# Four blocks instead of two share the opening phase of an attention and MoE kernel, with two sets of partial sums in DRAM

## The chip, the cores and the metric

One core of one Trainium2 chip runs the program. The metric is the device time of one execution in microseconds (us). PE is TensorE, DVE is VectorE, ACT is ScalarE, POOL is GpSimd, and SP is the engine whose queue issues most DMAs.

## What is computed

Attention over keys and values that are averaged in groups of 8 (576 positions become 72), then a dense two-layer MLP, then a mixture of 8 experts, of which each token uses the best one. Cut to what matters:

```
k_p, v_p = k.reshape(B,H,72,8,D).mean(3), v.reshape(B,H,72,8,D).mean(3)
x = softmax(q @ k_p.T / 8) @ v_p            # (8,8,576,64), as 4608 tokens x 512
h = x @ w_in                                # 512 -> 2048
y = maximum(0.01*h, h) @ w_out              # 2048 -> 512
e = argmax(y @ w_gate); p = softmax(y @ w_gate)[e]
out = p * (maximum(y @ w1[e], 0) @ w2[e])   # 512 -> 1024 -> 512
```

The inputs lie in DRAM; the weights `w_in` and `w_out` of the dense layer come as 64-bit floats.

## The kernel before

The 4608 tokens are cut into 18 blocks of 256 (`b`), and the 2048 columns of the dense layer into 16 pieces of 128 (`f`). A **slot** is one pair (b, f). The list `seq` sets the order of the slots, and each engine executes its instructions in program order. A slot `s` holds, in this order:

- `g1(b, f)`: 12 matmuls of 256 columns (x and weights are each split in a high and a low part, three products of the four are used) into a PSUM bank of tag `h`; ACT copies the bank times 0.01 into an SBUF tile `g`; DVE takes the maximum of the two.
- `g_lo` of the slot before (DVE), then what `hooks` planned for this slot (`at(slot, function)`): attention steps, key and value pooling, loads, evacuations.
- `g2` of two slots earlier: 6 matmuls of 512 columns into two PSUM banks `y`, which gather all 16 pieces of a block.
- `conv`: conversion of weight pieces. `w_load64` loads 512 KB, `w_conv1` takes 2 ACT and 4 DVE instructions to make fp32 of 64-bit words, `w_conv2` (1 ACT, 1 DVE) splits them into the two parts. There are 32 pieces: `w_in` and `w_out` for each f.
- `g_hi(b, f)` (ACT) makes the high part of the activation; `g_lo` (DVE) the low part.

So `g2` of a slot needs `g_lo`, which stands on DVE behind the maximum of the next slot, and that stands behind the conversion of its own slot.

In the **opening phase** the weights are not yet there. Blocks 0 and 1 go through it together: slots 0 to 3 are (0,0) to (0,3), then (0,f) and (1,f-4) alternate (LAG = 4), and slots 28 to 31 are (1,12) to (1,15). Block b = 2 begins at slot 32, and every later block takes 16 slots. An attention tile `t` (128 tokens) is made by `att_a` (PE transposes, ACT copy), `att_b` (scores; DVE maximum and subtraction), `att_e` (ACT exp), `att_n` (DVE sum, reciprocal, product), `att_c` (PE transposes, ACT and DVE splits); `att_av(b)` (PE, ACT, DVE) makes the block's x. After a block, `y_evac` copies y to SBUF on ACT and stores it to DRAM. Its gate logits are 16 DVE reductions (`logit`); only block 0 uses PE instead (`y_tr`, `y_logit`). From slot 34 on the expert weights are brought in 128 pieces through a ring of three SBUF buffers of tag `ps`: `ps_load` (SP), two slots later `ps_split` (ACT copy, POOL subtraction), one slot later `ps_store` (DMA issued by ACT). The ring hands out its buffers in program order, and a request waits until that buffer's last user is done. The expert steps begin after slot 287.

Of the kernel before, what the change touches and what calls it, by code (L numbers as in the profile page):

```python
# [21 lines left out]
def kernel(  # L22
# [13 lines left out]
    P = 128  # L36
# [3 lines left out]
    LAG = 4  # L40
    E, _, FE = moe2_w1.shape
# [24 lines left out]
    lst = dram.tile([(E * CAP + 1) * P, 2], F32, name="lst")  # L66
    wgT_d = dram.tile([E, DM], F32, name="wgT_d")
# [282 lines left out]
    def att_av(b):  # L350
        for g in range(2):
# [16 lines left out]
            xv = xs(b)  # L368
            act_copy(xv[:, ks, 0], pv)
            sub(nc.vector, xv[:, ks, 1], pv, f32(xv[:, ks, 0]))  # L370


    def w_load64():
        kind, f = w_todo.pop(0)
        r = r64[w_cnt[0] % len(r64)]
        w_cnt[0] += 1
# [39 lines left out]
    w_raw, w_mid, w_cnt = {}, {}, [0]  # L416
# [3 lines left out]
    def g1(b, f):  # L420
        p = pt("h")
        xv = xs(b)
        n = 0
        for kk in range(KD):
            for l, r in ((0, 0), (0, 1), (1, 0)):
                nc.tensor.matmul(  # L426
                    p[:, 0:BLK], win(f)[:, kk, l], xv[:, kk, r], start=(n == 0), stop=(n == 3 * KD - 1)
                )
                n += 1
        t = sb([P, BLK], F32, "g", 2)  # L430
        g = p[:, 0:BLK]
# [13 lines left out]
    def g2(b, f):  # L445
        hl = g_hl.pop((b, f))
        if f == 0:
            for i in range(TPB):
                y_ps[b, i] = bank(f"y{2 * (b == 1) + i}")
        last = f == NF - 1  # L450
        order = [(0, 0, 0), (0, 0, 1), (1, 0, 0), (1, 0, 1), (0, 1, 0), (1, 1, 0)]
        for i, l, r in order:
            nc.tensor.matmul(  # L453
                y_ps[b, i], hl[:, l, i * P:i * P + P], wout(f)[:, r], start=(f == 0 and l + r == 0),
                stop=(last and l == 1),
            )
# [367 lines left out]
    def plan():  # L824
        for t in range(4, NT // P):
# [9 lines left out]
        for b in range(2, NB):  # L835
            at((b - 1) * NF + NF - 1, att_av, b)
        for nb in range(2, B):
# [15 lines left out]
            at(max(use[0] - 6, 0), kv_load, nb, 0)  # L853
            at(use[0] - 5, kv_load, nb, 1)
        for i in range(E * NCH):
            s = 34 + i * 9 // 5
# [3 lines left out]
        for b in range(NB - 1):  # L860
            s = (b + 1) * NF + 1
            lg_at = []
            if b == 0:
                at(30, y_evac, 0)
                at(31, y_tr, 0, 0)
                at(32, y_tr, 0, 1)
                at(33, y_logit, 0)
                r = (34, 36)
            elif b == 1:
                ev, r = 37, (46, 48)  # L870
                lg_at = [38 + j // 2 for j in range(16)]
# [31 lines left out]
    def y_tr(b, i):  # L903
# [3 lines left out]
        tg = (("qT", 1), ("q", 1))[i] if b == NB - 1 else ("kv", 2)  # L907
        yT[i] = sb([P, KD, P], F32, *tg)
# [242 lines left out]
```

## Time and profile before

| | |
|---|---|
| time, median of 3 runs (lowest to highest) | 1575.14 us (1573.2 to 1575.79) |
| the profiled execution: its own time, its span | 1575.01 us, 1573.2 us |
| PE busy, DVE busy, ACT busy, POOL busy | 94%, 59%, 41%, 21% of the span |
| mean granted TensorE clock | 0.977 of full speed |

The time outside the span is 1.8 us. Matmuls are pipelined and the profile models their ends, so a busy PE does not mean a PE at its peak rate.

### The profile page before, as it was taken

How to read it: one execution, taken by the hardware profiler on the slowest of the kernel's cores; microseconds unless marked ns; L12 is line 12 of the kernel's file. 1: busy time of each engine (PE TensorE's matmuls, PEld its weight loads, DVE VectorE, ACT ScalarE, POOL GpSimd, SP SyncE). 2: the span in 40 equal slices, each digit the busy share in tenths (PEclk: the TensorE clock that was granted, in tenths of full speed). 3: DMA queues.
4: the chain of work that ended last, by engine and by line, in shares of the span. 5: the costliest groups of instructions: out<-in, count | busy, mean ns of one | idle time of the engine just before them, and what ended most of it. 6: DMA issues, size and time to landing. Idle time of an engine off the chain costs nothing. (4 is left out here: it accounts for less than half of the span.)

```text
span 1573.2 us, 25017 instructions
## 1 busy us (share of the span) xinstructions
PE 1478.4 (94%) x8778; PEld 1292.1 (82%) x8778; DVE 929.4 (59%) x2393; ACT 643.2 (41%) x1444; POOL 329.6 (21%) x290
## 2 busy tenths in 40 slices
PE   4567899999999999999999999999999999999998
PEld 3456689999898888899889899987888888888886
DVE  6989748978788879877878878653111111111111
ACT  4655544445444454544445444322222222222222
POOL 3000002232332233222222333021111111121111
PEclk8787999999999999999999999999999999999999
DMA  8533035656555555545636554054721331661160
GB/s 208 159 108 102 28 127 174 183 166 196 152 178 170 180 160 184 179 157 166 198 135 198 165 162 160 28 212 160 292 111 48 147 145 41 228 278 46 61 235 22
DMA packets 113280, 238.01 MB, mean 151 GB/s; under 512 B 47589, under 2 KB 55785, under 8 KB 109440
## 3 DMA queue, kind: packets, MB, share of 16 engines
q1 hardware_dynamic: 82208, 139.81, 28.5%
q10 hardware_dynamic: 23328, 76.56, 13.1%
q0 software_dynamic: 7616, 20.01, 3.9%
q8 instruction: 71, 1.16, 0.4%
q14 instruction: 57, 0.47, 0.2%
HBM read 418.44 MB, written 87.38 MB: 322 GB/s over the span
## 5 line engine op out<-in xcount | busy, mean ns | idle before, releaser
L453 PE MATMUL y<-w,ghl 128*128 128x512 f32 x1728 | 464.3, 406 | 0.4 <-DVE ghl L126 0.2
L453 PEld LDWEIGHTS y<-w,ghl 128*128 128x128 f32 x1728 | 311.0, 192 | 56.5 <-DVE ghl L126 1.7
L426 PEld LDWEIGHTS h<-x_t,w 128*128 128x128 f32 x1776 | 237.5, 196 | 58.9 <-issue 21.7
L426 PE MATMUL h<-x_t,w 128*128 128x256 f32 x1776 | 245.6, 289 | 40.8 <-ACT ghl L123 21.4
L126 POOL TENSOR_TENSOR ps<-ps 128x512 f32<-128x512 f32 x128 | 182.7, 1427 | 479.8 <-ACT ps L123 356.5
L473 DVE CUSTOM_DVE_ANT_0 junk<-y,wg 128x512 bf16<-128x512 f32 x256 | 197.9, 773 | 1.9
L426 PEld LDWEIGHTS y<-x_t,w 128*128 128x128 f32 x1488 | 189.6, 188 | 9.4
L426 PE MATMUL y<-x_t,w 128*128 128x256 f32 x1488 | 192.1, 280 | 0.0
L126 DVE TENSOR_TENSOR at_t<-a,at_t 128x512 fp32r<-128x512 f32 x76 | 52.4, 689 | 203.8 <-ACT at_t L123 203.6
L126 DVE TENSOR_TENSOR vm<-a,vm 128x512 fp32r<-128x512 f32 x40 | 27.7, 692 | 199.7 <-ACT vm L123 199.7
L123 ACT ACTIVATE g<-h 128x256 f32<-128x256 f32 x164 | 62.9, 383 | 173.0 <-PE h L426 162.4
L433 DVE TENSOR_TENSOR h<-g,h 128x256 f32<-128x256 f32 x164 | 69.5, 424 | 91.6 <-ACT g L123 91.0
L797 PE MATMUL y<-w,at_t 128*128 128x512 f32 x480 | 120.8, 400 | 1.4 <-ACT at_t L123 0.9
L805 POOL DMA_INDIRECT out_dram<-kv,sidx x40 | 40.3, 1008 | 382.7 <-ACT vm L123 192.3
L797 PE MATMUL y<-w,vm 128*128 128x512 f32 x480 | 120.3, 400 | 0.0
L771 PE MATMUL h<-w,x_t 128*128 128x512 f32 x480 | 118.5, 396 | 0.0
L771 PE MATMUL y<-w,x_t 128*128 128x512 f32 x480 | 118.4, 395 | 0.0
L123 ACT ACTIVATE ghl<-h 128x256 fp32r<-128x256 f32 x164 | 62.7, 382 | 111.3 <-PE y L453 46.7
L797 PEld LDWEIGHTS y<-w,at_t 128*128 128x128 f32 x480 | 88.6, 188 | 22.0 <-ACT at_t L123 1.2
L797 PEld LDWEIGHTS y<-w,vm 128*128 128x128 f32 x480 | 88.7, 188 | 20.1
L771 PEld LDWEIGHTS h<-w,x_t 128*128 128x128 f32 x480 | 88.7, 188 | 18.8 <-DVE x_t L126 0.4
L771 PEld LDWEIGHTS y<-w,x_t 128*128 128x128 f32 x480 | 88.6, 188 | 18.4
(238 smaller groups left out, 1906.4 us busy)
## 6 DMA issues: line engine op xcount, KB each, us to landing
w<-wsp SPq DMA_DIRECT2D x156, 2048.0 KB
wsp<-ps ACTq DMA_DIRECT2D x128, 512.0 KB
ps<-in_moe_w_dram SPq DMA_DIRECT2D x128, 256.0 KB
y_d<-y ACTq DMA_DIRECT2D x18, 512.0 KB
q<-in_q_dram SPq DMA_DIRECT2D x28, 256.0 KB
kv<-in_k_dram SPq DMA_DIRECT2D x24, 288.0 KB
kv<-in_v_dram SPq DMA_DIRECT2D x24, 256.0 KB
ps<-in_moe_w_in_dram SPq DMA_DIRECT2D x8, 512.0 KB
```

The source lines that it names most:

```text
L123: nc.scalar.activation(o, i, AF.Copy, scale=scale)
L126: eng.tensor_tensor(out=o, in0=a, in1=b, op=ALU.subtract)
L426: nc.tensor.matmul(p[:, 0:BLK], win(f)[:, kk, l], xv[:, kk, r], start=(n == 0), stop=(n == 3 * KD - 1))
L433: nc.vector.tensor_tensor(out=g, in0=t, in1=g, op=ALU.max)
L453: nc.tensor.matmul(y_ps[b, i], hl[:, l, i * P:i * P + P], wout(f)[:, r], start=(f == 0 and l + r == 0), stop=(last and l == 1),)
L473: nc.vector.tensor_tensor_reduce(out=jk, in0=y_sb[b][:, i], in1=wg_t[0][:, e], scale=1.0, scalar=0.0, op0=ALU.mult, op1=ALU.add, accum_out ...
L771: nc.tensor.matmul(p, xT2[:, t % 2, kk, l], wlane(lane(t), fh * KD + kk)[:, r], start=(n == 0), stop=(n == 3 * KD - 1))
L797: nc.tensor.matmul(p, d[:, kk, l], wlane(lane(t), 2 * KD + 4 * j + kk)[:, r], start=(j == 0 and n == 0), stop=(j == 1 and n == 11),)
L805: nc.gpsimd.indirect_dma_start(out=out, out_offset=bass.IndirectOffsetOnAxis(ap=sidx[:, t:t + 1], axis=0), in_=o, in_offset=None, bounds_c ...
```

## The change

- `seq`: `pair(0, 8)` runs blocks 0 and 1 through f = 0 to 7 (slots 0 to 15), `pair(2, 16)` runs blocks 2 and 3 through all 16 pieces (slots 16 to 47), then come (0, 8..15) in slots 48 to 55 and (1, 8..15) in slots 56 to 63. From slot 64 (block 4) on the order is that of before.
- `cv_at` sets the slot in which each piece is converted: n = 2 to 9 two in a slot in slots 0 to 3, n = 10 to 15 one in each of slots 4 to 9, none in slots 10 to 14, n = 16 to 31 in slots 15 to 39, eight steps of slots for five pieces. There are 5 load buffers instead of 7, and 3 from n = 18 on.
- The y sums of blocks 0 and 1 after f = 7 are copied to SBUF by ACT and stored to DRAM (`y_part`, slots 13 and 18), loaded again (`part_load`, slots 53 and 61, in the `ps` ring) and added by DVE in `y_evac`.
- The activation of blocks 0 to 3 stays in the SBUF tile `g`, no longer in the PSUM bank `h`.
- Attention tiles 4 to 7 and `att_av(2)`, `att_av(3)` move up into slots 7 to 19. Pooling for batch 1 moves up by 2 to 5 slots.
- Blocks 1 to 3 get their gate logits from PE as block 0 does. `y_tr` takes its tile from the `ps` ring. The expert weights start at slot 42 instead of 34, the gate rows for later blocks are loaded after slot 63 instead of slot 31.

```diff
+
+    def w_load64(n):
+        f, kind = divmod(n, 2)
+        r = r64[n % 5 if n < NK else (n - NK) % 3]
         if kind == 0:
             src = moe_w_in.bitcast(I32)[:, 2 * P * f:2 * P * f + 2 * P].rearrange("(a p) c -> p a c", p=P)
...
-        act_copy(t, g, 0.01)
-        nc.vector.tensor_tensor(out=g, in0=t, in1=g, op=ALU.max)
+        h = p[:, 0:BLK]
+        g = t if b < NQ else h
+        act_copy(t, h, 0.01)
+        nc.vector.tensor_tensor(out=g, in0=t, in1=h, op=ALU.max)
         g_raw[b, f] = g

     def g_hi(b, f):
@@ -444,16 +446,31 @@
...
-        if f == 0:
+        first = f == 0 or (b < 2 and f == NF // 2)
+        last = f == NF - 1 or (b < 2 and f == NF // 2 - 1)
+        if first:
             for i in range(TPB):
-                y_ps[b, i] = bank(f"y{2 * (b == 1) + i}")
-        last = f == NF - 1
...
+                y_ps[b, i], hl[:, l, i * P:i * P + P], wout(f)[:, r], start=(first and l + r == 0),
                 stop=(last and l == 1),
             )
+
+    part = {}
+
+    def y_part(b):
+        if b == 0:
+            part["sb"] = sb([P, 2, TPB, DM], F32, "w03")
+        t = part["sb"][:, b]
+        for i in range(TPB):
+            act_copy(t[:, i], y_ps.pop((b, i)))
+        nc.sync.dma_start(out=part_d[b], in_=t)
+
+    def part_load(b):
+        part[b] = sb([P, TPB, DM], F32, "ps", 3)
+        nc.sync.dma_start(out=part[b], in_=part_d[b])

...
         for i in range(TPB):
-            act_copy(y[:, i], y_ps.pop((b, i)))
+            p = y_ps.pop((b, i))
+            if b in part:
+                nc.vector.tensor_tensor(out=y[:, i], in0=part[b][:, i], in1=p, op=ALU.add)
+            else:
+                act_copy(y[:, i], p)
         nc.scalar.dma_start(
...
     seq = []
-    for i in range(NF + LAG):
-        if i < NF:
-            seq.append((0, i))
-        if i >= LAG:
-            seq.append((1, i - LAG))
-    seq += [(b, f) for b in range(2, NB) for f in range(NF)]
+
+    def pair(b, n):
+        for i in range(n + LAG):
+            if i < n:
+                seq.append((b, i))
+            if i >= LAG:
+                seq.append((b + 1, i - LAG))
+
+    pair(0, NF // 2)
+    pair(2, NF)
+    seq += [(b, f) for b in range(2) for f in range(NF // 2, NF)]
+    seq += [(b, f) for b in range(NQ, NB) for f in range(NF)]
+    slot = {x: s for s, x in enumerate(seq)}
...
-        for t in range(4, NT // P):
+        for t, ss in ((4, (7, 8, 9, 10, 12)), (5, (10, 11, 12, 13, 14)), (6, (12, 13, 14, 14, 16)), (7, (15, 16, 17, 17, 18))):
+            for fn, c in zip((att_a, att_b, att_e, att_n, att_c), ss):
+                at(c, fn, t)
+            at(ss[0], q_load, t + 1)
+        at(15, lambda: x_of.update({2: [sb([P, 2, 2, BLK], F32R, "kv", 2) for g in range(2)]}))
+        at(15, att_av, 2)
+        at(19, att_av, 3)
...
+            if nb == 2:
+                use = [48, 51, 53, 56]
             use += [use[3] + 2, use[3] + 4, use[3] + 6]
...
         for i in range(E * NCH):
-            s = 34 + i * 9 // 5
+            s = 42 + i * 9 // 5
...
-            elif b == 1:
-                ev, r = 37, (46, 48)
-                lg_at = [38 + j // 2 for j in range(16)]
+            if b < NQ:
+                e = slot[b, NF - 1] + 3
+                if b != 1:
+                    at(e, y_evac, b)
+                at(e + 1, y_tr, b, 0)
+                at(e + 2, y_tr, b, 1)
+                at(e + 3, y_logit, b)
+                r = (e + 4, e + 6)
+                if b < 2:
+                    at(slot[b, NF // 2 - 1] + 3, y_part, b)
+                    at(e - 5, part_load, b)
...
-        yT[i] = sb([P, KD, P], F32, *tg)
+        if b == NB - 1:
+            yT[i] = sb([P, KD, P], F32, ("qT", "q")[i])
+        else:
+            if i == 0:
+                yT["ps"] = sb([P, TPB, KD, P], F32, "ps", 3)
+            yT[i] = yT["ps"][:, i]
...
-
-        def load2():
-            for _ in range(2):
-                if w_todo:
-                    w_load64()
+        x_of.update({0: xa[0], 1: xa[1]})
...
+            w_conv1(n % 2, n // 2)
+
+        def conv2(n):
+            w_conv2(n % 2, n // 2)
+            for m in (n + 3, n + 5):
+                if m < 2 * NF and (m >= NK) == (m == n + 3):
+                    w_load64(m)

         kv_load0_k(0)
         q_load(0)
...
+        cv_at = {}
+        for n in range(2, 2 * NF):
+            c = n // 2 - 1 if n < 10 else n - 6 if n < 16 else 15 + (n - 16) * 8 // 5
+            cv_at.setdefault(c, []).append(n)
+
+        def conv(s):
+            for n in cv_at.get(s, []):
+                conv2(n)
+            for n in cv_at.get(s, []):
+                if n + 2 < 2 * NF:
+                    conv1(n + 2)
...
-            end = s >= 2 * NF - 1 and (s % NF == NF - 1 or s % NF == 0)
+            end = s >= NQ * NF - 1 and (s % NF == NF - 1 or s % NF == 0)
             while len(pend) > (1 if end else 2):
                 g2(*pend.pop(0))
-            if s < 2 * NF:
-                conv(s, b, f)
-            if b > 2 and f == 0:
-                y_evac(b - 1)
-            if (b, f) == (2, 6):
+            conv(s)
+            if b >= NQ and f == 0:
+                y_evac(b - 1 if b > NQ else 1)
+            if (b, f) == (NQ, 3):
                 banks["h"] += ["y2", "y3"]
             g_hi(b, f)
-            if s < 2 * NF + LAG - 1:
+            if s < NQ * NF - 1:
                 late.append((b, f))
             else:
                 g_lo(b, f)
```

DVE in the stretch in which weights are converted. Before, slot 9 and the start of slot 10; a row with `h_` at the left is the maximum of a slot, `ghl` is `g_lo`, `w_` and the four rows after it are one piece's `w_conv2` and `w_conv1`.

```order
L433 TENSOR_TENSOR h_808<-g,h_808 128x256
L126 TENSOR_TENSOR ghl<-h_767,ghl 128x256
L126 TENSOR_TENSOR w_576<-ps,w_576 128x512
L393 SCALAR_TENSOR_TENSOR e_106<-y_111,e_106 128x512
L396 TENSOR_SCALAR y_111<-y_111 128x512
L399 SCALAR_TENSOR_TENSOR y_111<-y_111 128x512
L402 TENSOR_TENSOR y_111<-y_111,e_106 128x512
L433 TENSOR_TENSOR h_842<-g,h_842 128x256
L126 TENSOR_TENSOR ghl<-h_808,ghl 128x256
```

Now, slots 20 and 21 and the start of slot 22; the maximum is the row with `g<-g,h_`.

```order
L435 TENSOR_TENSOR g<-g,h_1402 128x256
L128 TENSOR_TENSOR ghl<-g,ghl 128x256
L435 TENSOR_TENSOR g<-g,h_1428 128x256
L128 TENSOR_TENSOR ghl<-g,ghl 128x256
L128 TENSOR_TENSOR w_1190<-ps,w_1190 128x4x128
L394 SCALAR_TENSOR_TENSOR y_109<-ps,y_109 128x512
L397 TENSOR_SCALAR ps<-ps 128x512
L400 SCALAR_TENSOR_TENSOR ps<-ps 128x512
L403 TENSOR_TENSOR ps<-ps,y_109 128x512
L435 TENSOR_TENSOR g<-g,h_1462 128x256
L128 TENSOR_TENSOR ghl<-g,ghl 128x256
```

Before, nearly each slot of this stretch held a piece; now every second or third slot holds none, and the maximum writes the SBUF tile `g`.

PE at slot 16 and the start of slot 17. Before, `h_1077<-x_t` is `g1` of block 0 with columns 8 to 11 (`w_872`), `h_1126<-x_102` that of block 1 with columns 4 to 7, `L287` begins attention tile 4, the rows with `y_` are `g2`.

```order
L426 MATMUL h_1077<-x_t,w_872 128x256 x12
L287 MATMUL a_1100<-ident,q 128x128 x4
L453 MATMUL y_508<-w_907,ghl 128x512 x2
L453 MATMUL y_509<-w_907,ghl 128x512 x2
L453 MATMUL y_508<-w_907,ghl 128x512
L453 MATMUL y_509<-w_907,ghl 128x512
L426 MATMUL h_1126<-x_102,w_572 128x256 x12
```

Now, where `kv` holds the x of block 2, and `L340` to `L308` are attention tiles 6 and 7.

```order
L427 MATMUL h_1202<-kv,w_295 128x256 x12
L340 MATMUL a_1219<-ident,pn 128x128 x4
L346 MATMUL a_1226<-ident,pn 32x128 x2
L308 MATMUL a_1234<-kT_72,qT 128x144 x2
L308 MATMUL a_1239<-kT_72,qT 128x144 x2
L456 MATMUL y_778<-w_585,ghl 128x512 x2
L456 MATMUL y_779<-w_585,ghl 128x512 x2
L456 MATMUL y_778<-w_585,ghl 128x512
L456 MATMUL y_779<-w_585,ghl 128x512
L427 MATMUL h_1262<-kv,w_295 128x256 x12
```

In place of block 0's later columns PE has block 2 with the weights `w_295` of columns 0 to 3, which were converted for slots 0 to 3, and attention steps between.

The SP queue in slots 51 to 56, after the change; `L712` is `ps_load`, `L282` a load of q, `L176`, `L183` and `L190` loads of k and v.

```order
L176 DMA kv<-in_k_dram 72x2x512
L712 DMA ps<-in_moe_w_dram 128x512 x2
L183 DMA kv<-in_v_dram 64x2x512 x2
L473 DMA ps<-part_d 128x1024
L712 DMA ps<-in_moe_w_dram 128x512
L282 DMA q<-in_q_dram 128x8x64
L183 DMA kv<-in_v_dram 64x2x512 x2
L712 DMA ps<-in_moe_w_dram 128x512
```

The row `L473`, block 0's partial sums, takes a buffer of the `ps` ring between two pieces of the expert weights, and rows behind it in the queue wait until it is issued.

## Rows read from the trace of the kernel before

**Rows 1.** The page: busy tenths of TensorE and its clock in 40 equal slices.
```profile
PE   4567899999999999999999999999999999999998
...
PEclk8787999999999999999999999999999999999999
```
**Rows 2.** Windows of six stretches: length, busy PE, PEld, DVE, ACT, POOL, then PEclk.
```profile
36.60:108.90 72.30, 44.14 (x222) 37.55 (x222) 66.26 (x128) 43.65 (x83) 0.00 (x0) 0.81 0.47 137
108.90:132.30 23.40, 18.20 (x92) 15.33 (x92) 22.30 (x45) 13.98 (x30) 0.00 (x0) 0.85 0.37 113
132.30:159.40 27.10, 20.58 (x111) 17.65 (x111) 24.02 (x49) 15.14 (x33) 1.89 (x1) 0.81 0.36 108
159.40:210.40 51.00, 44.29 (x286) 38.16 (x287) 34.13 (x71) 25.93 (x55) 0.68 (x3) 1.00 0.18 63
210.40:251.10 40.70, 38.42 (x264) 34.79 (x263) 27.23 (x89) 16.50 (x39) 8.58 (x7) 1.00 0.45 129
251.10:320.90 69.80, 68.53 (x463) 62.61 (x462) 60.73 (x163) 34.94 (x88) 18.95 (x15) 1.00 0.55 168
```
**Rows 3.** VectorE in order of time, one conversion of a piece: start, us, instruction.
```profile
104.85 0.68 DVE L126 TENSOR_TENSOR w<-ps,w 128x512 fp32r<-128x512 f32 x1
...
107.36 0.69 DVE L402 TENSOR_TENSOR ps<-ps,e 128x512 uint32<-128x512 uint32 x1
107.97 0.42 DVE L433 TENSOR_TENSOR h<-g,h 128x256 f32<-128x256 f32 x1
```
**Rows 4.** VectorE groups by form, 0 to 205 us: busy, mean ns | idle before.
```profile
L433 DVE TENSOR_TENSOR h<-g,h 128x256 f32<-128x256 f32 x32 | 13.6, 424 | 15.6 <-ACT g L123 15.6
...
L312 DVE TENSOR_REDUCE st<-a 128x4 f32<-128x288 f32 x8 | 3.6, 453 | 4.3 <-PE a L306 4.3
...
L322 DVE TENSOR_REDUCE st<-pr 128x8 f32<-128x576 f32 x4 | 3.0, 743 | 0.0
...
L126 DVE TENSOR_TENSOR at_t<-a,at_t 128x512 fp32r<-128x512 f32 x6 | 4.1, 682 | 0.0
```
**Rows 5.** VectorE groups by form, whole span: the gate logits.
```profile
L473 DVE CUSTOM_DVE_ANT_0 junk<-y,wg 128x512 bf16<-128x512 f32 x256 | 197.9, 773 | 1.9
```
**Rows 6.** Waits of all engines, 0 to 350 us: total, times, longest.
```profile
DVE h L433 <- ACT g L123: 34.1, 22, 3.8
...
PE h L426 <- ACT ghl L123: 21.4, 9, 3.3
```
**Rows 7.** TensorE in order of time, two steady slots.
```profile
278.48 1.58 PE L426 MATMUL h<-x_t,w 128*128 128x256 f32 x12
...
281.25 1.58 PE L426 MATMUL y<-x_t,w 128*128 128x256 f32 x12
```
**Rows 8.** TensorE in order of time, block 0's logits on TensorE.
```profile
207.19 0.60 PE L906 MATMUL a<-ident,y 128*128 128x128 f32 x4
207.54 3.05 PE L453 MATMUL y<-w,ghl 128*128 128x512 f32 x12
...
215.51 1.85 PE L915 MATMUL a<-wgk,kv 128*128 128x8 f32 x16
217.22 1.62 PE L426 MATMUL h<-x_t,w 128*128 128x256 f32 x12
```
**Rows 9.** ScalarE groups by form, 0 to 205 us: copies and a conversion step.
```profile
L392 ACT ACTIVATE e<-junk,ebias 128x512 uint32<-128x512 uint16 x32 | 23.1, 723 | 1.0
L123 ACT ACTIVATE g<-h 128x256 f32<-128x256 f32 x32 | 12.2, 382 | 44.9 <-PE h L426 44.8
...
L123 ACT ACTIVATE w<-ps 128x512 fp32r<-128x512 f32 x15 | 10.0, 668 | 0.9 <-DVE ps L402 0.7
...
L123 ACT ACTIVATE y<-y 128x512 f32<-128x512 f32 x2 | 1.1, 599 | 0.0
```
**Rows 10.** Waits of the SP queue, 300 to 1000 us.
```profile
SPq L691 <- DMA wsp<-ps: 242.1, 64, 9.5
```
**Rows 11.** Waits of ScalarE, 210 to 1000 us.
```profile
ACT ps L123 <- DMA ps<-in_moe_w_dram: 15.1, 15, 2.5
```

More of the change, by code (lines that the diff above doesn't have):

```diff
@@ L40 @@
     LAG = 4
+    NQ = 4
     E, _, FE = moe2_w1.shape
@@ L66 @@
     lst = dram.tile([(E * CAP + 1) * P, 2], F32, name="lst")
+    part_d = dram.tile([2, P, TPB, DM], F32, name="part_d")
     wgT_d = dram.tile([E, DM], F32, name="wgT_d")
@@ L421, in g1 @@
         p = pt("h")
-        xv = xs(b)
         n = 0
         for kk in range(KD):
+            x = x_of[b][kk // 2][:, kk % 2] if b in x_of else x_v[:, kk]
             for l, r in ((0, 0), (0, 1), (1, 0)):
                 nc.tensor.matmul(
-                    p[:, 0:BLK], win(f)[:, kk, l], xv[:, kk, r], start=(n == 0), stop=(n == 3 * KD - 1)
+                    p[:, 0:BLK], win(f)[:, kk, l], x[:, r], start=(n == 0), stop=(n == 3 * KD - 1)
                 )
@@ L824, in plan @@
     def plan():
-        for t in range(4, NT // P):
+        for t, ss in ((4, (7, 8, 9, 10, 12)), (5, (10, 11, 12, 13, 14)), (6, (12, 13, 14, 14, 16)), (7, (15, 16, 17, 17, 18))):
[5 more added lines that the diff above has]
+        at(19, att_av, 3)
+        for t in range(8, NT // P):
             b, i = divmod(t, TPB)
@@ L834, in plan @@
             at(s + 5, att_c, t)
-        for b in range(2, NB):
+        for b in range(4, NB):
             at((b - 1) * NF + NF - 1, att_av, b)
@@ L922, with conv1 @@
         start = stack.enter_context(tc.tile_pool(name="start", bufs=1))
-        x1 = start.tile([P, KD * 2 * BLK], F32R, name="x1")
+        xa = [[start.tile([P, 2, 2, BLK], F32R, name=f"xa{b}{g}") for g in range(2)] for b in range(2)]
         ebias = sb([P, 1], F32, "ebias")
         nc.vector.memset(ebias, -114688.0 * 65536.0)
-        e_t = [start.tile([P, 512], U32, name=f"e{i}") for i in range(2)]
+        e_2 = sb([P, 2, 512], U32, "y4")
+        e_t = [e_2[:, i] for i in range(2)]
         ab_t = sb([P, 512], BF16, "junk")
         r64 = [sb([P, 1024], I32, "ps", 3) for i in range(3)]
-        r64.append(sb([P, 1024], I32, "y4"))
-        r64.append(start.tile([P, 1024], I32, name="r64"))
         r64 += [sb([P, 1024], I32, "kv", 2) for i in range(2)]
+        NK = 18
         q0 = sb([P, 4, H, D], F32, "w12")
         alt = sb([P, 4096], F32, "w02")
-        x_of = {1: x1.rearrange("p (k h n) -> p k h n", k=KD, h=2)}
-        w_todo = [(j, f) for f in range(NF) for j in range(2)]
-        def xs(b):
-            return x_of.get(b, x_v)
-        def load2():
-            for _ in range(2):
-                if w_todo:
-                    w_load64()
+        x_of.update({0: xa[0], 1: xa[1]})
+        def conv1(n):
+            w_conv1(n % 2, n // 2)
[4 more added lines that the diff above has]
+                    w_load64(m)
         kv_load0_k(0)
@@ L948 @@
         kv_load0_v(0)
-        load2()
-        load2()
+        for n in range(4):
+            w_load64(n)
         q_load(2)
         q_load(3)
-        w_load64()
+        w_load64(4)
         consts()
@@ L975 @@
         kv_use(0, 6)
-        w_conv2(0, 0)
-        w_conv1(1, 0)
+        conv2(0)
+        conv1(1)
         att_av(0)
-        w_conv2(1, 0)
+        conv2(1)
         kv_load0_k(1)
-        w_load64()
         kv_load0_v(1)
-        load2()
-        w_conv1(0, 1)
-        w_conv1(1, 1)
-        for i, c in enumerate((6, 8, 10, 12, 14, 15, 16)):
+        conv1(2)
+        conv1(3)
+        for i, c in enumerate((4, 5, 6, 7, 9, 11, 13)):
             at(c - 2, kv_pool, 1, i)
```

49 lines of the change are left out of this document (12 added, 37 removed).

## Prediction

> **What bounds the kernel now.** The page comes first: TensorE is busy for 9 tenths or more of each slice of 39.3 us from the sixth to the last but one, and for 4 to 8 tenths in the first five, where its clock begins at 7 to 8 tenths [rows 1]. What an opening phase can win lies there, and the slots that the change moves end with slot 63, at 320.9 us. I cut that stretch at the starts of slots 0, 10, 15, 20, 32, 44 and 64 (36.6, 108.9, 132.3, 159.4, 210.4, 251.1 and 320.9 us), the six lines of [rows 2], and set VectorE against TensorE.
>
> *Stage A, slots 0 to 19:* 72.3 + 23.4 + 27.1 = 122.8 us, VectorE busy for 66.3 + 22.3 + 24.0 = 112.6 us of it. VectorE is the bound. Its 10.2 us of idle time are waits for the ACT copy of `g` (34.1 us in all up to 350 us), and TensorE in its turn waited 21.4 us for `g_hi` to read the `h` bank [rows 6]: a loop between engines through a bank that is held long.
>
> *Stage B, slots 20 to 43:* 51.0 + 40.7 = 91.7 us at full clock, VectorE busy for 61.4 us only. *Stage C, slots 44 to 63:* 69.8 us, TensorE busy for 68.5.
>
> The rate of a TensorE that is not held up: `g1` of one slot to `g1` of the next, with one `g2` between, is 281.25 - 278.48 = 2.77 us [rows 7]; I take 2.80. The matmuls of 64 slots are 179 us of the 284 between 36.6 and 320.9.
>
> **The change, part by part.** Work of a slot is counted from the order of the program, with start-to-start durations of the trace. For the kernel before this gives VectorE 112.1 us in stage A, against 112.6 busy; so the method holds.
>
> *Stage A.* One converted piece is 107.97 - 104.85 = 3.12 us of VectorE [rows 3]. Slots 0 to 19 convert 18 pieces instead of 24: -18.7 us. They take over tiles 4 to 7, of which one scores step was there: a tile is two maxima and two subtractions at 0.45, sum and product at 0.74 and about 0.9, small ones 0.4, two splits 0.68 and about 0.4 [rows 4], 4.9 us, so +17.9. Two more `att_av` are four splits of 0.62, +2.5. Sum +1.7: VectorE has 114 us there, as much as now. By parts: slots 0 to 9 have 71.6 (6.3 more, four pooling steps of batch 1 and tile 4), 10 to 14 17.6, 15 to 19 24.2. TensorE has 10.6 us more there (tiles and `att_av`) and comes to 70 at full clock, in the two short parts 17.1 and 21.4. For the idle time: blocks 0 to 3 free the `h` bank after the maximum, so `g1` can run one step earlier, and most of the waits on `g` should go in the slots that VectorE bounds; in slots 10 to 19 the engines are level and will wait for each other. I take 75 + 20 + 26 = 121, gain 2. Bounds: 116 (sums without idle), 130 (the idle share of today, and the clock staying at 0.82 so that TensorE needs 38.5/0.82 = 47 us in slots 10 to 19).
>
> *Stage B* is where the gain lies. Nothing of attention is left on TensorE there: 24 x 2.80 + 0.4 = 67.6 us. VectorE has 12 splits and 10 first conversions, together 33 us, and 24 times maximum and `g_lo`, 17 us: 50 us. TensorE is the bound if no slot is late. A slot with a piece costs VectorE 0.7 + 3.1 = 3.8 us, more than 2.8; one without costs 0.7. Single slots catch up. In two in a row (slots 23 and 24, 26 and 27, 31 and 32, 34 and 35) ACT's copy of `g`, the split, two conversion steps of 0.7 each [rows 9] and four VectorE steps stand ahead of the second slot's maximum; from the end of the first `g1` I count 9.8 us to the `g_lo` that `g2` needs at 8.4. So 1.4 us four times, 73 us in all: gain 18.7. Bounds: 67.6, and 77.2 if each slot takes its longer engine.
>
> *Stage C.* The second half of blocks 0 and 1 takes the place of blocks 2 and 3 as slots. TensorE: logits of three blocks, by 2 x 0.35 + 1.71 = 2.4 each from starts [rows 8], +7.2; tiles and `att_av` that moved up, about -4. It has 70 us, and I add 3 for waits: 73.2 against 69.8, a loss of 3.4. Bounds: 70 and 78.
>
> *Behind slot 64:* block 1's logits, +2.4. 48 VectorE reductions of 0.77 us [rows 5], 37 us, fall away, and are worth nothing where TensorE is the bound.
>
> *Costed at nothing.* Partial sums: four ACT copies of 0.60 [rows 9] and 2 MB in all to and from DRAM, in slots 13, 18, 53 and 61, each five slots or more before the use; ACT is at 56% in slots 15 to 19. If that cover is gone a copy costs its 0.6 us. The two additions per block move from ACT to VectorE, 0.7 each. Expert weights eight slots later: done by slot 273, read from slot 281. The gate rows, 2 MB, now enter SP's queue at slot 63 among the expert weights; at the 168 GB/s that stage C moves [rows 2] they take 12 us and are read 17 slots later, while a `ps_load` behind them has two slots: up to 6 us for ACT if they went first, inside rival 3. `g_hi` now reads SBUF: 0.668 against 0.599 us for 512 columns [rows 9], so up to 0.07 x 64 = 4.5 us of ACT, hidden by ACT's idle half.
>
> [...]
>
> Sum: -2 - 18.7 + 3.4 + 2.4 = -14.9 from the profiled execution's 1575.0 (span 1573.2 and 1.8 around it), which is the median of the three runs to 0.1 us. **Predicted: 1560 us.** By the lower bounds -7 - 24 + 0 + 2 = -29, 1546; by the upper +7 - 14.5 + 8 + 3 = +3.5, 1579.
>
> **The rivals.**
>
> 1. *Bunched conversions hold TensorE through stage B and attention through C:* each slot takes the longer of its engines. That is 77.2 in B and 78 in C: -2 - 14.5 + 8 + 2.4 = -6, 1569. For it: the same rule gives 280 us for slots 0 to 63 of the kernel before, which took 284. Against it: there the bank was held until `g_lo`.
> 2. *The opening stays as long:* stage A takes over attention of two blocks, its chains of five steps through three engines stand in slots 7 to 19, and TensorE's clock remains at 0.82. Stage A grows by 13 and eats the gain: 1573 to 1577. For it: VectorE's work there does not shrink. Against it: steps lie one to three slots apart.
> 3. *Slower: the `ps` ring.* Four logit tiles and two partial sums take buffers from three that the expert weights rotate, in slots 46 to 67, some 21 requests where there were 15. SP already waits for a store's end 64 times, 3.8 us on average, 9.5 at most [rows 10], and ACT for a load 15 times, up to 2.5 us [rows 11]. An inserted `y_tr` copy waits on ACT itself, with `g_hi` and the next `g` behind it, and through `g_lo` PE. Six times 3.8 us is 23: 1560 + 23 = 1583. It decides from 2.5 us for each on. Against it: in most cases the buffer was stored a slot or more earlier, and a slot without conversion has some 1.6 us to spare.
>
> **Chances.** Forecast (1550 to 1569) 0.55; rival 1 0.20; rival 2 0.12; rival 3 0.13. A change of under 0.2% (3.2 us) cannot be told from none in this kernel. Faster: nearly all of the forecast and rival 1, a quarter of rival 2, a little of rival 3, 0.77. Same: 0.10, mostly rival 2. Slower: 0.13, mostly rival 3. The range, 1546 to 1579, takes in the bounds above and leaves out the greater part of rival 3.
>
> **What would show it.** In the changed kernel's windows slot 20 should begin near 158 us, slot 44 near 231, slot 64 near 304 (now 159.4, 251.1, 320.9). VectorE should be 93% busy or more in slots 0 to 9. In slots 20 to 43 TensorE should be over 90% busy at full clock, its waits short ones on `g_lo`, four or so. The waits on `g_hi` for the bank should be nearly gone. In slots 46 to 67 ACT should show no waits for a DMA or for POOL above 2 us. I am wrong if slot 20 begins after 170 us (attention chains, clock), if slots 20 to 43 take 80 us or more (bunching, or loads that arrive late, since from n = 18 on a piece's load is issued only one conversion ahead), or if stage C takes over 85 (the ring).

## The result and the profile after

The changed kernel takes 1593.59 us (median of 4 runs, 1593.50 to 1593.73), the kernel before 1575.47 beside it: ratio 1.0111, interval 1.0087 to 1.0135. It is slower by 18 us where 15 us less were forecast. The stages tell where, in the profiled execution (span 1591.8 us, against 1573.2). The page of the changed kernel, the two lines that answer [rows 1]:

```profile
PE   4587889799999999999999999999999999999998
...
PEclk7589999989999999999999999999999999999999
```

TensorE's share now dips in the eighth slice too, and its clock in the ninth (318 to 358 us). The windows of the changed kernel, cut at the starts of slots 0, 10, 15, 20, 32, 44 and 64, then at the first ACT copies of the x of block 5 and of block 17, which are called the activations of these blocks here and in the expectations (columns as in [rows 2]):

```profile
36.97:108.10 71.13, 48.49 (x243) 42.12 (x244) 65.57 (x128) 42.40 (x85) 0.00 (x0) 0.71 0.47 130
108.10:139.80 31.70, 23.20 (x127) 19.83 (x126) 24.66 (x59) 14.64 (x34) 1.12 (x2) 0.84 0.17 50
139.80:167.00 27.20, 22.72 (x163) 20.93 (x162) 20.36 (x43) 16.88 (x35) 0.00 (x0) 1.00 0.27 83
167.00:206.40 39.40, 34.99 (x221) 30.35 (x220) 32.10 (x64) 21.23 (x47) 0.00 (x0) 1.00 0.32 98
206.40:243.70 37.30, 34.47 (x217) 30.26 (x216) 24.10 (x58) 17.29 (x38) 0.59 (x2) 1.00 0.27 83
243.70:336.90 93.20, 81.86 (x516) 73.86 (x515) 49.05 (x146) 38.00 (x94) 21.41 (x17) 0.91 0.46 143
336.90:394.80 57.90, 54.06 (x352) 49.47 (x351) 28.65 (x84) 21.98 (x54) 14.55 (x12) 0.94 0.64 187
394.80:1024.40 629.60, 624.92 (x4211) 570.81 (x4211) 512.22 (x1384) 305.58 (x748) 179.72 (x134) 0.99 0.55 172
```

The last two stretches in the kernel before:

```profile
320.90:368.30 47.40, 47.40 (x326) 43.64 (x325) 36.69 (x104) 22.20 (x54) 13.57 (x11) 1.00 0.55 183
368.30:1006.00 637.70, 627.84 (x4213) 572.13 (x4213) 515.55 (x1404) 303.25 (x747) 181.37 (x133) 0.99 0.52 166
```

| stretch | before | forecast | changed | against before |
|---|---|---|---|---|
| A, slots 0 to 19 | 122.8 | 121 | 130.0 | +7.2 |
| B, slots 20 to 43 | 91.7 | 73 | 76.7 | -15.0 |
| C, slots 44 to 63 | 69.8 | 73.2 | 93.2 | +23.4 |
| slot 64 to block 5's activations | 47.4 | +2.4 | 57.9 | +10.5 |
| block 5's to block 17's activations | 637.7 | 637.7 | 629.6 | -8.1 |

With 0.4 us ahead of slot 0 and 0.2 behind the last stretch these make the 18.6 us between the spans. B came nearly as forecast, C lost it all and more, and behind slot 64 a loss and a gain that were both not forecast nearly cancel. Waits up to 350 us in the changed kernel, which answer [rows 6]:

```profile
DVE g L435 <- ACT g L125: 53.8, 26, 6.5
...
PE y L456 <- DVE ghl L128: 10.7, 8, 1.8
```

TensorE has no wait on `g_hi` for the bank any more (21.4 us before). VectorE's waits for the ACT copy of `g` grew from 34.1 us to 53.8; ACT in its turn waited 33.3 us in the same stretch for the `g1` matmuls. The worst place is slot 61. First TensorE there, then ACT, then SP's queue, all of the changed kernel in order of time (idle time and its releaser in brackets):

```profile
308.91 1.58 PE L427 MATMUL h<-xa,w 128*128 128x256 f32 x12
310.33 0.60 PE L340 MATMUL a<-ident,pn 128*128 128x128 f32 x4
316.63 0.61 PE L346 MATMUL a<-ident,pn 128*32 128x128 f32 x2 [5.70 <-ACT ps L125]
318.60 3.58 PE L956 MATMUL a<-wgk,ps 128*128 128x8 f32 x16 [1.36 <-DVE at_t L128]
322.04 2.91 PE L456 MATMUL y<-w,ghl 128*128 128x512 f32 x6
324.74 2.76 PE L427 MATMUL h<-xa,w 128*128 128x256 f32 x12
```
```profile
315.46 0.63 ACT L125 ACTIVATE ps<-ps 128x512 fp32r<-128x512 f32 x1 [5.23 <-DMA ps<-in_moe_w_dram]
```
```profile
307.67 0.35 SPq L712 DMA_DIRECT2D ps<-in_moe_w_dram  x1
```

ACT waits 5.2 us at the split of an expert weight piece. SP issued its load at 307.67, and it is there at 315.4. TensorE waits behind ACT (5.70), then for the bank of its logits (1.36), and then works at half clock (granted 0.50 from 318.6 to 327.4 us): the six `g2` matmuls take 2.91 us (1.64 in the last row shown of E9, below), the `g1` 2.76 instead of 1.58 [rows 7]. This one slot takes 15.8 us.

### The profile page after: what moved, and what is told of

The parts are those of the page before. It is cut to its first block, busy times and chain, and to the rows that moved or that the text cites. A ratio compares the mean times of both kernels' runs of the same rounds, so it can differ in the third digit from the quotient of the medians.

```text
span 1591.8 us, 25118 instructions
## 1 busy us (share of the span) xinstructions
PE 1493.8 (94%) x8850; PEld 1307.5 (82%) x8850; DVE 900.2 (57%) x2304; ACT 646.2 (41%) x1450; POOL 323.5 (20%) x290
## 5 line engine op out<-in xcount | busy, mean ns | idle before, releaser
L128 POOL TENSOR_TENSOR ps<-ps 128x512 f32<-128x512 f32 x128 | 178.9, 1397 | 497.1 <-ACT ps L125 423.7
L427 PEld LDWEIGHTS h<-x_t,w 128*128 128x128 f32 x1560 | 201.3, 189 | 12.3 <-DVE ghl L128 1.3
L427 PE MATMUL h<-x_t,w 128*128 128x256 f32 x1560 | 204.6, 281 | 1.1 <-DVE ghl L128 1.1
L427 PEld LDWEIGHTS y<-x_t,w 128*128 128x128 f32 x1320 | 169.4, 190 | 8.5
L427 PE MATMUL y<-x_t,w 128*128 128x256 f32 x1320 | 171.6, 281 | 0.0
L494 DVE CUSTOM_DVE_ANT_0 junk<-y,wg 128x512 bf16<-128x512 f32 x208 | 168.3, 809 | 1.4
L125 ACT ACTIVATE g<-h 128x256 f32<-128x256 f32 x178 | 68.1, 382 | 140.7 <-PE h L427 129.5
L818 PEld LDWEIGHTS y<-w,at_t 128*128 128x128 f32 x480 | 88.6, 188 | 21.9 <-ACT at_t L125 1.2
L792 PEld LDWEIGHTS y<-w,x_t 128*128 128x128 f32 x480 | 88.6, 188 | 18.4
L125 ACT ACTIVATE ps<-ps 128x512 fp32r<-128x512 f32 x128 | 80.4, 628 | 26.5 <-DMA ps<-in_moe_w_dram 21.3
L435 DVE TENSOR_TENSOR h<-g,h 128x256 f32<-128x256 f32 x114 | 48.3, 424 | 63.7 <-ACT g L125 63.3
```

What stands on the lines that cost most here:

```text
L125: nc.scalar.activation(o, i, AF.Copy, scale=scale)
L128: eng.tensor_tensor(out=o, in0=a, in1=b, op=ALU.subtract)
L427: nc.tensor.matmul(p[:, 0:BLK], win(f)[:, kk, l], x[:, r], start=(n == 0), stop=(n == 3 * KD - 1))
L435: nc.vector.tensor_tensor(out=g, in0=t, in1=h, op=ALU.max)
L494: nc.vector.tensor_tensor_reduce(out=jk, in0=y_sb[b][:, i], in1=wg_t[0][:, e], scale=1.0, scalar=0.0, op0=ALU.mult, op1=ALU.add, accum_out ...
L792: nc.tensor.matmul(p, xT2[:, t % 2, kk, l], wlane(lane(t), fh * KD + kk)[:, r], start=(n == 0), stop=(n == 3 * KD - 1))
```

## The experiments

Sixteen kernels; in those with more than a line changed, line numbers shift by a few. Stage times are those of each profiled execution, cut at the same slots. Ratios are to the kernel before, executed beside each of them; its own executions lay between 1566 and 1582 us, so small differences are better read from ratios than from medians. Single stages vary too: in five kernels whose edits are not in stage C (E3, E4, E6, E8, E13) C took 89.2 to 91.9 us, against 93.2 in the changed kernel.

**E1, expert weights later.**
```
-            s = 42 + i * 9 // 5
+            s = 68 + i * 8 // 5
```


> The expert weights (load, split, store through the ps buffers) start at slot 68 instead of slot 42, at a pace of 1.6 slots instead of 1.8, so that in slots 44 to 67 only the logit tiles and the partial sums ask for ps buffers. Theory (the ps ring): slots 44 to 63 take 72 to 78 us instead of 93.2, ACT's and POOL's waits for the ps loads in slots 46 to 64 go, and the time falls by 15 to 20 us, to 1574 to 1579; the faster pace behind slot 68 may take back up to 3. Rival (stage C is long because it holds the logits of three blocks and the attention of blocks 4 at a lower clock): slots 44 to 63 still take 88 us or more and the time stays within 5 us of 1593.6.

1580.59 us, ratio to before 1.0036 (1.0019 to 1.0053). C took 83.5 us, slot 64 to block 5's activations 51.6 instead of 57.9, the later blocks 632.9. The weight pieces cost some 10 us in C (6 to 8 against the five kernels above) and 6 behind it, but C misses both bands: another 10 us have another cause. It shows at 257 us, and again at 309; between them, at 278, block 3's logits stand free of waits:

```profile
256.66 0.23 PE L243 MATMUL a<-ident,kv 72*128 72x72 f32 x1
257.51 2.21 PE L956 MATMUL a<-wgk,ps 128*128 128x8 f32 x16 [0.62 <-ACT qT L125]
259.58 2.91 PE L456 MATMUL y<-w,ghl 128*128 128x512 f32 x6
...
278.85 1.89 PE L956 MATMUL a<-wgk,ps 128*128 128x8 f32 x16
280.60 1.64 PE L456 MATMUL y<-w,ghl 128*128 128x512 f32 x6
...
309.22 2.67 PE L956 MATMUL a<-wgk,ps 128*128 128x8 f32 x16 [1.71 <-DVE at_t L128]
311.74 2.91 PE L456 MATMUL y<-w,ghl 128*128 128x512 f32 x6
```

The logit matmuls of blocks 2 and 0 wait 0.62 and 1.71 us for the bank that an attention step took just ahead, and the next `g2` takes 2.91 us, as at the granted clock of 0.50 in slot 61 above.

**E2, own buffers for the ring's guests.** The core of the diff (the memory of block 3's activations takes block 3's logit tile and block 0's partial sums, that of block 0 takes its logit tile and block 1's partial sums; the gate rows' load moves back one slot with them):
```
-        part[b] = sb([P, TPB, DM], F32, "ps", 3)
+        part[b] = part["x"] if b == 0 else start.tile([P, TPB, DM], F32, name="xa01", tag="xa01")
...
+            if i == 0 and b == 0:
+                yT["ps"] = start.tile([P, TPB, KD, P], F32, name="xa00", tag="xa00")
+            elif i == 0 and b == 3:
+                r = sb([P, 2, TPB, DM], F32, "x_t")
```


> The expert weights stay where they are; the logit tiles of blocks 3 and 0 and both partial sums leave the ps ring for memory that is idle there (the activations' buffers of block 3 and of block 0). Block 2's logit tile (slot 46) and block 1's (slot 67) stay in the ring. Theory (requests beside the expert weights in a ring of three): slots 44 to 63 take 73 to 80 us instead of 93.2 and the time falls by 13 to 20 us, to 1574 to 1581. Rival (the expert weights' loads, splits and stores are themselves what stage C cannot carry next to three blocks of logits, whoever shares the ring): slots 44 to 63 still take 86 us or more.

1597.02 us, 1.0144 (1.0113 to 1.0175), C 89.7, in the rival's band. The guests that moved out are not what stalls the ring: ACT still waits 3.7 us for a weight piece at slot 61 (3.0 to 3.7 in the five kernels above, which keep them). Block 2's and block 1's logit tiles stayed in it.

**E3, batch 1's keys and values on POOL's queue.**
```
-            nc.sync.dma_start(out=kt[:, hs], ...
+            (nc.gpsimd if nb else nc.sync).dma_start(out=kt[:, hs], ...
...
```


> The keys and values of batch 1 are loaded by POOL's queue instead of SP's, where their last eight descriptors stood from 40.9 to 55.8 us ahead of the weight loads. Theory (late weight loads lengthen slots 2 to 4): the 7.6 us wait of ACT for a weight load near 61 us goes, slot 10 begins at 103 us or earlier (108.1 in the changed kernel), slot 20 at 163 or earlier, and the time falls by 4 to 8 us. Rival (VectorE's work and the attention chains set the opening): slot 10 may come earlier, but slot 20 stays within 2 us of 167.0, and so does the time of 1593.6.

1587.19 us (1585.37 to 1591.46), 1.0080 (1.0051 to 1.0108). ACT's 7.6 us wait is gone, slot 10 comes at 104.7, slot 20 at 165.2: of 3.4 us gained 1.6 are given back by slot 20. That is the rival's band for slot 20 and the theory's for the median, but slot 10 misses the theory's 103. In the profiled execution late loads are under 2 of the 9 us by which A exceeds its forecast; it is the longest of the four, and where the others gain more no profile shows. In the changed kernel SP's queue stood 14.9 us at these loads, with the weight loads behind:

```profile
40.91 14.93 SPq L212 DMA_DIRECT2D w<-in_v_dram  x8
```

The eight issues take 2.4 of the 14.9 us themselves, the rest is waits between them in the queue (12.3 us, until earlier loads had ended), and in E3 the next weight load is issued at 45.9 us instead of 57.3. By slot 20 the gain is a small 1.8 us all the same.

**E4, attention steps one slot apart.**
```
-        for t, ss in ((4, (7, 8, 9, 10, 12)), (5, (10, 11, 12, 13, 14)), (6, (12, 13, 14, 14, 16)), (7, (15, 16, 17, 17, 18))):
+        for t, ss in ((4, (7, 8, 9, 10, 13)), (5, (10, 11, 12, 13, 15)), (6, (13, 14, 15, 16, 18)), (7, (15, 16, 17, 18, 19))):
```


> The steps of tiles 4 to 7 stand one slot further apart: the transposes of tiles 4, 5 and 7 one slot later, those of tile 6 two, its other steps one. Theory (in slots 10 to 14 TensorE waits for chains of attention steps that stand too close): slots 10 to 19 take 53 us or less instead of 58.9, the waits of the transposes for VectorE (10 us) go, slot 20 begins at 161 or earlier and the time falls by 5 to 8 us. Rival (VectorE's backlog from slots 2 to 9 and the late loads set it): slots 10 to 19 within 2 us of 58.9.

1593.85 us, 1.0133 (1.0100 to 1.0166). Slots 10 to 14 fall to 28.0, slots 15 to 19 rise to 35.3: 63.3 together instead of 58.9. The wait moves to the end, where block 3's activations need tile 7 (3.6 us). That is outside both bands: the theory's cure fails, and the rival isn't shown by it.

**E5, E1 without three blocks' logits.**
```
+        if b in (0, 2, 3):
+            nc.vector.tensor_copy(lg[b], y_sb[b][:, :, 0:E])
+            return
```


> On top of the first experiment (expert weights from slot 68): the transposes and gate matmuls of blocks 2, 3 and 0 are left out, and their logits are eight columns of y instead, so that tokens go to other experts; what counts is the time up to slot 64, not the total. It prices the logits of three blocks inside slots 44 to 63, which took 83.5 us in the first experiment. Theory (the logits cost much more than the 7.2 us of matmuls, through waits around them and through TensorE's clock, which stood at half after two of the three): slots 44 to 63 take 72 us or less. Rival (the attention steps of blocks 4's tiles and the key and value steps of batch 2 hold it): they take 76 us or more, and the clock still falls near slot 61.

C took 66.9 us, 16.6 less than in E1, at full clock. Windows of C in E1 and in E5:

```profile
242.70:326.20 83.50, 79.80 (x515) 72.49 (x514) 44.81 (x146) 31.54 (x82) 5.14 (x5) 0.94 0.30 85
```
```profile
246.60:313.50 66.90, 66.39 (x443) 60.51 (x442) 44.23 (x146) 27.96 (x76) 5.75 (x5) 1.00 0.38 106
```

The theory holds. Three logit tiles cost 5.5 us each, not 2.4, and without them the half clock is gone (granted 1.00 instead of 0.94).

**E6, gate rows in quarters, and 5 to 14 slots later.**
```
...
-                    in_=wgT_d.rearrange("e d -> (e d)").partition_broadcast(P),
+                for i in range(4):
+                    at(NQ * NF + 4 + 3 * i, wg_load, i)
```


> As the changed kernel, with the 2 MB of gate rows loaded in four quarters at slots 68, 71, 74 and 77 instead of in one at the end of slot 63. Theory (the gate rows' transfer delays the weight load behind it, on which ACT waited 6.2 us near 355 us, and that lengthens slots 64 to 79): from the first activations of block 4 to those of block 5 it takes 57 us or less instead of 62.4, and the time falls by 4 to 6 us. Rival (block 1's logit tile in the ps ring and the split's place on ACT do that, whatever the gate rows do): 61 us or more, and the time within 2 us of 1593.6.

1585.14 us (1579.53 to 1591.07), 1.0076 (1.0049 to 1.0103). Block 4's activations to block 5's take 55.9 us. The theory holds: the time falls by 8.4 between the medians and by 5.5 by the ratios, where it said 4 to 6. Whether the smaller loads or their later slots do it, the run doesn't separate.

**E7, `g` in the bank again.**
```
-        g = t if b < NQ else h
+        g = h
```


> As the changed kernel, but the maximum g stays in the h bank for blocks 0 to 3 as it did before, so that the bank is held until the low part is taken. It tells what the freed bank is worth. Theory of the prediction (the freed bank lets g1 run ahead, and that carries the gain of slots 20 to 43): those slots take 83 us or more instead of 76.7, slots 0 to 19 are 3 us or more longer, and the time rises by 8 us or more. Rival (the gain of slots 20 to 43 comes from attention and conversions that moved away, and the bank is worth little): they take 79 us or less and the time rises by less than 3 us.

1604.46 us, 1.0188 (1.0168 to 1.0209). B takes 88.6 us, slot 20 comes 3.7 us later, and TensorE's `g1` waits again, 14.7 us in B. The theory holds. The freed bank is worth 12 of the 15 us gained in B.

**E8, pieces spread.**
```
-            c = ... else 15 + (n - 16) * 8 // 5
+            c = ... else 13 + (n - 16) * 15 // 8
```


> As the changed kernel, with the last 16 converted pieces spread from slot 13 on by 15/8 slots instead of from slot 15 by 8/5, so that two adjacent slots with a piece come twice instead of five times. Theory (adjacent pieces make VectorE late for the low part, 1.2 to 1.8 us each): slots 20 to 43 take 72 us or less instead of 76.7; the two pieces that move to slots 13 and 14 cost nothing or up to 2 us there, and the time falls by 2 to 5 us. Rival (waits in slots 20 to 43 come from the pieces' loads, or the work moved ahead lengthens slots 10 to 19 by as much): no gain in the time.

1585.92 us (1578.05 to 1588.38), 1.0073 (1.0051 to 1.0094). B takes 69.2 us, TensorE's waits for the low part fall from 7.2 us (5) to 0.9 (1); slot 20 comes 1.4 us later. The theory holds; the time falls by 7.7 between the medians and by 6.0 by the ratios, a little more than it said.

**E9, E1 with the logit steps first in their slots.**
```
     def plan():
+        for b in range(NQ):
+            e = slot[b, NF - 1] + 3
+            at(e + 3, y_logit, b)
...
```


> As the first experiment (expert weights from slot 68), with one more change: in a slot that has logit steps of blocks 0 to 3 these stand directly behind g1 and ahead of the attention and key steps, so that the logit matmuls no longer wait for a bank that an attention step has just taken. Same work. Theory (of the 16.6 us that the logits of three blocks cost in slots 44 to 63, some 8 are matmuls, and the rest is those waits and the half clock behind them): slots 44 to 63 take 74 to 77 us instead of 83.5, the granted clock there is 0.98 or more instead of 0.94, and the time falls from 1580.6 to about 1573. Rival (the clock falls because of the logit matmuls themselves, with 8 columns each, wherever they stand, or the wait passes to the attention steps): 81 us or more.

1572.37 us (10 runs), 0.9999 (0.9982 to 1.0017). C takes 74.9 us with the same work as E1's 83.5. Its window, and the same place as in E1:

```profile
245.10:320.00 74.90, 74.47 (x516) 68.29 (x515) 44.98 (x146) 31.70 (x82) 5.14 (x5) 1.00 0.35 95
```
```profile
258.65 1.85 PE L958 MATMUL a<-wgk,ps 128*128 128x8 f32 x16
260.35 0.64 PE L289 MATMUL a<-ident,q 128*128 128x128 f32 x4
260.82 0.23 PE L243 MATMUL a<-ident,kv 72*128 72x72 f32 x1
260.85 1.64 PE L456 MATMUL y<-w,ghl 128*128 128x512 f32 x6
```

No wait, and `g2` at 1.64. So of the 16.6 us 8.0 are the work (7.2 were counted) and 8.6 waits and half clock: idle time of TensorE falls from 3.7 to 0.4 us, busy time from 79.8 to 74.5. The theory holds, and the rival (narrow matmuls lower the clock wherever they stand) falls: the same matmuls leave the clock at 1.00.

A short wait does not settle the clock either. Block 2's logits wait 0.62 us in the changed kernel too, and there the next `g2` is at full clock (1.00):

```profile
258.56 1.95 PE L956 MATMUL a<-wgk,ps 128*128 128x8 f32 x16 [0.62 <-ACT qT L125]
260.36 1.65 PE L456 MATMUL y<-w,ghl 128*128 128x512 f32 x6
```

The changed kernel and E1 to E4 all have this wait of 0.62 us at this place. The `g2` behind it takes 2.91 us in E1 and 2.62 in E4, and 1.64 to 1.65 in the changed kernel, E2 and E3. In the same five, block 0's logits wait 1.36 to 1.71 us, in all but E1 behind a longer wait (3.5 to 5.7 us), and each time the next `g2` takes 2.91 us. What decides after 0.62 us stays open.

**E10 and E11, all together,** with late weights (diffs of E1, E3, E8, E9) and with weights at slot 42 and the gate rows in quarters (E3, E6, E8, E9).

> All together: expert weights from slot 68, keys and values of batch 1 on POOL's queue, converted pieces spread from slot 13, logit steps first in their slots. If the parts add up (slots 0 to 19 shorter by 2, slots 20 to 43 by 7, slots 44 to 63 by 17 and slots 64 to 79 by 6, the later blocks longer by 3 for the faster pace of the expert weights) the time is 1593.6 - 29 = 1565, faster than both kernels (ratio 0.993). If each stage's gain is met by a new wait, as in the fourth experiment, it stays at 1573 or above.

> The same with the expert weights left at slot 42 and the gate rows in quarters behind slot 67. Theory (the stall near slot 61 is a weight split that waits on ACT for its load, with or without the logits' place): slots 44 to 63 remain 6 to 10 us longer than in the kernel with late weights, the later blocks are some 3 us shorter, and the time is 1568 to 1573. Rival (the ring's stall only bites where the logits wait too, so that it goes with the new order): slots 44 to 63 within 3 us of the other kernel and the time at 1565 or less.

E10: 1562.04 us (6 runs, 1558.41 to 1565.09), 0.9940 (0.9918 to 0.9961). E11: 1563.13, 0.9942 (0.9920 to 0.9964). Both beat both kernels. In E10 the parts add up. C takes 74.8 and 80.2 us, so that in E11 the weight pieces still cost 5 us there, between the two bands; its time is in the rival's. These 5 us are TensorE's idle time (5.2 us in E11, 0.4 in E10); the clock is at 1.00 in both.

**E12, the kernel before with one number changed.**
```
-            s = 34 + i * 9 // 5
+            s = 42 + i * 9 // 5
```


> The kernel before, with one number changed: its expert weights start at slot 42 instead of slot 34, at the same pace, as in the changed kernel. It tells where the changed kernel got back some 8 us behind slot 80: the stretch from the first activations of block 5 to those of block 17 takes 637.7 us in the kernel before and 629.6 in the changed one. Theory (the phase in which the weight pieces meet the key, value and attention steps): that stretch falls to 632 or less, and the time by up to 8 us if slots 42 to 80 lose nothing. Rival (something else that the change does to the later blocks): it stays at 635 or more.

1563.41 us (6 runs, 1561.10 to 1564.39), 0.9921 (0.9891 to 0.9951). Slot 64 starts 1.3 us earlier, and the stretch of blocks 5 to 16 falls from 637.7 to

```profile
367.10:993.90 626.80, 622.11 (x4213) 568.05 (x4212) 516.89 (x1404) 304.85 (x750) 180.35 (x136) 1.00 0.54 172
```

The theory holds, with more than the 8 us that it said, and the kernel before with this one number is as fast as E10 and E11. Two things make up the stretch's 10.9 us. TensorE is idle for 4.7 us instead of 9.9, and two spells at half clock (793.5 to 800.3 and 902.7 to 906.1 us in the kernel before, granted 0.50 and 0.51) are gone; 10.2 us at half clock cost about 5, an estimate from the granted clock. Why this phase suits the foreground better, no run shows.

**E13, tiles 6 and 7 left out.**
```
-                at(c, fn, t)
...
+                if t < 6:
+                    at(c, fn, t)
...
```


> As the changed kernel, with the attention steps of tiles 6 and 7 (slots 12 to 18) left out, so that block 3 gets the values of block 2's tiles; what counts is the time up to slot 20. Slots 10 to 19 took 58.9 us, where 46 were forecast, with VectorE busy for 45.0 and TensorE for 45.9. The two tiles are 9.8 us of VectorE's work and about 4 of TensorE's. Theory (chains of attention steps make the two engines wait for each other): slots 10 to 19 fall by more than VectorE's share, to 46 us or less. Rival (VectorE arrives late from slots 0 to 9, and its work sets the rest): they fall by 10 us at most, to 49 or more.

Slots 10 to 19 took 48.3 us, 10.6 less, between the bands. VectorE was busy 9.0 us less, and its idle time there stays at 12.3 us (13.9 in the changed kernel). That speaks for VectorE's work and against these two chains, but doesn't settle it. The total doesn't count, since block 3's values are not its own.

**E14, E11 with E2's buffers.** 

> As the eleventh experiment (expert weights from slot 42, gate rows in quarters, logit steps first, spread pieces, keys and values on POOL's queue), with the logit tiles of blocks 3 and 0 and both partial sums out of the ps ring, as in the second. Slots 44 to 63 took 80.2 us there and 74.8 with late expert weights. Theory (logit tiles and partial sums beside the expert weights in the ring cost those 5 us, and the second experiment hid it behind the logits' waits): slots 44 to 63 take 76 us or less and the time is 1557 to 1560. Rival (the expert weights' own loads behind the key and value loads stall it): 79 us or more, and the time within 2 us of 1563.

1568.48 us, 0.9941 (0.9928 to 0.9955). C takes 83.9 us, ACT waits 5.3 us for one piece. By the ratio the time is E11's. The guests that moved are cleared a second time.

**E15, E11 with block 0's `y` stored four slots later; E16, E11 with the split one slot later.**
```
+        at(slot[0, NF - 1] + 7, y_store, 0)
```
```
-            at(s + 2, ps_split, i)
+            at(s + 3, ps_split, i)
```


> As the eleventh experiment, with the 512 KB store of block 0's y put four slots later (slot 62 instead of 58), out of the place where eight small value loads, a 512 KB store of a weight piece and the next piece's load meet. In the changed kernel that load took 7.8 us to land, and ACT waited 5.2 us for it. Theory (the y store delays that load): ACT's wait of 3 to 5 us for a weight piece near slot 60 goes, slots 44 to 63 take 77 us or less instead of 80.2, and the time falls by 2 to 4 us. Rival (the store of the piece and the small value loads are enough): the wait stays and the time is within 2 us of the eleventh's.

> As the eleventh experiment, with the split of each weight piece one slot later (in the slot of its store), so that a load has three slots to land instead of two. Theory (late loads stall TensorE only because ACT takes up the split two slots behind the load's place): ACT's waits for weight pieces near slot 60 go, slots 44 to 63 take 77 us or less instead of 80.2; the later blocks may lose up to 5 us, since the ring turns more slowly and loads are issued later. Rival (ACT waits as long, one slot later): 79 us or more.

E15: 1566.52 us, 0.9944 (0.9917 to 0.9972), C 80.8, and ACT still waits 2.4 us there: the `y` store is not it. E16: 1611.12 us, 1.0221 (1.0190 to 1.0252), C 84.3. ACT's waits for the weight loads near slot 60 are gone, but C is no shorter, and blocks 5 to 16 take 670.3 us instead of 628.4. ACT's waits from 400 to 1000 us:

```profile
ACT ghl L125 <- POOL ps L128: 77.9, 32, 4.7
```

The store of a piece is issued by ACT and needs POOL's half of the split. With the split in the same slot, ACT waits for POOL there, and `g_hi` stands behind it.

## Why the prediction was wrong

*The main step that failed* is stage C: "It has 70 us, and I add 3 for waits". The waits and the half clock, for which 3 us stood, took 18.3 us (93.2 against the 74.9 of E9, which lacks both causes): 9.7 by the weight pieces (E1; 6 to 8 against the five kernels whose edits are not in C), then 8.6 by the logits' place (E9). With the logits first, the weight pieces cost 5 (E10, E11), so the shares depend on the order. I counted each `y_logit` by its starts in [rows 8], where it stood free of waits, and not by what its bank waits for in its new slots. The 70 us of work were too few as well: the prediction's own 68.5 + 7.2 - 4 is 71.7, and where neither the pieces nor the logits' place disturb C (E9) TensorE is busy for 74.5 of 74.9 us, at full clock.

*Rival 3* (the `ps` ring, 1583) had the right sign, place and sort of wait, and the prediction's own mark for it came true (C over 85). Its mechanism is half wrong: the two logit tiles and two partial sums that were taken out of the ring had cost nothing that these runs can tell (E2, E14); the pieces stall with their own late loads. What makes such a load take 7.8 us stays open: neither own buffers nor the `y` store (E15) is it, and one slot more (E16) brings another wait.

*Stage B* went as argued in its mechanism. The bank carries 12 us of the gain (E7), waits for the low part behind adjacent pieces cost 7.2 us, forecast 5.6 (E8), and TensorE is busy for 69.5 us, forecast 67.6: 76.7 against 73, inside the bounds, and nearly rival 1's 77.2 for this stage.

*Stage A* ended at its upper bound, 130. VectorE's work was right (110.6 us busy, 114 counted), slots 0 to 9 were better than forecast (71.1 against 75), and slots 10 to 14 took 31.7 instead of 20. VectorE brought work along from slots 0 to 9 (24.7 us busy there, 17.6 counted) and stood idle for 7.0. Late loads explain under 2 us (E3). The rest looks like mutual waiting of level engines, which is argued and not shown; E4 and E13 don't settle which wait leads. Rival 2 had A grow by 13; it grew by 7.2.

*Behind slot 64* +2.4 forecast and +2.4 measured agree by accident: +10.5 and -8.1. The gate rows' load, put inside rival 3 at "up to 6 us", costs 6 of the first (E6). The reading of SBUF by `g_hi`, put at up to 4.5 us of ACT, costs 2.0: 416 ns from `g`, 385 from the bank (medians in the changed kernel), 64 times. And "Expert weights eight slots later", costed at nothing, is worth 11 us in the kernel before (E12), nearly all in blocks 5 to 16.

*Net:* the change by itself is probably worse than its 18 us, since 8 us of the lucky shift seem to be in it; this is argued from E12, as no run gives the changed kernel the old phase. And with most of its stalls repaired (E10, E11) it only equals the old opening with the same shift (E12).

## What to carry to other kernels

A step that moves brings its waits with it: price it from its new neighbours (whose bank, whose in-order engine, whose clock), not from starts where it stood free. Block 0's logits took 1.85 us in the kernel before [rows 8] and 3.58 behind a wait of 1.36 in the changed one. Put short steps that share banks with longer chains first in their slot (worth 8.6 us of C here, E9). Background work at a steady pace has a phase (worth 11 us here, E12): try a shift of it alone first, or a change that shifts it by the way is credited with the shift.

## What the runs showed of the hardware that was not expected

Waits of 1.36 to 1.71 us ahead of 16 narrow matmuls were followed by half clock in five kernels of five (the changed one, E1 to E4: `g2` 2.91 us instead of 1.64), a wait of 0.62 us in two of the five (2.91 us in E1, 2.62 in E4); the same matmuls without a wait were not (E9), and C ran at 1.00 there instead of 0.94 in E1. A 256 KB load landed after 7.8 us, issued 2 and 3.4 us behind two 512 KB stores; the cause stays open. And eight slots of phase of the weight pieces moved 1575 us by 11 (E12): TensorE was busy 5.7 us less for the same matmuls (627.8 to 622.1) and idle 5.2 us less.
